# Strassen's scheme for the first expert product of an attention + mixture-of-experts kernel

## The chip, the cores and the metric

One core of a Trainium2 chip. The metric is the device time of one execution in microseconds: median 1120.63 of three runs (1118.05 to 1121.13) for the kernel before. Engines are named as in the profile: PE (matmul) with its weight loads PEld, DVE (vector), ACT (scalar), POOL (GpSimd, which also issues the indirect transfers) and SP (which issues the plain ones).

## What is computed

Attention (8 batches, 8 heads, 576 positions, 64 wide; four heads with a window of 32, four with a dilated one) gives x, 4608 tokens of 512. A gate with noise picks the best two of eight experts for each token, and the experts' outputs are added with the two weights:

```python
for e in range(E):
    for k in range(2):
        mask = top2[:, k] == e
        if not mask.any():
            continue
        h = np.maximum(x[mask] @ w1[e], 0.0)
        out[mask] += top2_w[mask, k, None] * (h @ w2[e])
```

w1[e] is 512 x 1024, w2[e] is 1024 x 512, all float32. "First product" below is x @ w1, "second product" is h @ w2.

## The kernel before, in words

**Stages.** The attention, the gate and the lists of tokens take the first 235 us or so and are not touched, but for the place where the first expert's weights are prepared. Then come the experts one after the other, the fullest first, with fixed capacities of 1216 (three experts), 1184 (two) and 1152 rows (three): nine tiles of 128 rows, and 64, 32 or no rows more. A loop at the end, which runs only if an expert overflows its capacity, is not entered here.

**Precision.** Each float32 operand is split into a high part that the fast float32 matmul reads (fp32r) and a low part, the difference. ACT makes the high part by a cast, DVE the low part by a subtraction. A product is three matmuls: high x high, high x low, low x high.

**First product** (`up`, L814). An expert's rows stand in three blocks of 384, 512 and the remaining 256 to 320 rows. For each block and each of eight groups of 128 hidden columns, twelve matmuls (4 slices of the inner dimension x 3) go into one bank of PSUM, tile `up`, of which there are three. Then ACT rectifies it into `hh` (L818) and DVE makes `hl` (L820; L823 for a last partial tile).

**Second product** (`down_tile`, L856). For each tile of 128 rows, 24 matmuls of 512 columns (8 x 3) into tile `dn`; DVE scales it by the token's weight into `y` (L865), POOL adds it to the output rows by an indirect transfer (L833).

**The rows of x.** POOL gathers them tile by tile (L758 for expert 0, L766 for the others, four gathers a tile); PE (`xrp`, L780, expert 0) or DVE (`xr`, L783) transposes; ACT casts (L785), DVE subtracts (L786). **Weights** come over SP into two staging buffers `ws` (L686 W1, L700 W2, 512 KB a transfer), ACT casts (L694, L707), DVE subtracts (L696, L709).

**What sets the order.** Each engine runs its instructions in the order in which the program wrote them. The program keeps a clock of its own, `now`, which `tick` moves on by the columns of the matmuls just written; `plan(t, f)` writes a piece of side work when the clock has passed t. So gathers, casts and loads stand between the matmuls' follow-up work at places worked out from this clock. The order of blocks is by hand: first products of one expert and second products of the one before alternate. Slots of expert 0 are dealt out in three parts, SPLITS = (0, 384, 896): the first 384 slots are filled from the first half of the tokens, the next up to 896 after the third quarter, and the rest at the end, so that expert 0 can begin early.

Of the kernel before, what the change touches and what calls it, by code (L numbers as in the profile page):

```python
# [35 lines left out]
NWARM = 24  # L36
SL_W1 = 5
# [9 lines left out]
def attention_moe_kernel(ctx, tc, qt, kp, kd, vpl, vdl, w_gate, w_noise, noise, w1, w2, out, CAPS=(1216, 1216, 1216, 1184, 1184, 1152, 1152, 1152), SPLITS=(0, 384, 896)):  # L47
# [13 lines left out]
    NBL = [max(bl[i][3] for bl in BLS) for i in range(3)]  # L61
# [11 lines left out]
    gp_ = ctx.enter_context(tc.tile_pool(name="gp", bufs=4))  # L73
# [180 lines left out]
    def setup_c():  # L254
# [3 lines left out]
        free = [late["stage"].tile([128, FF], I32, name="free", tag="ws") for _ in range(2)]  # L258
# [421 lines left out]
    ST = {}  # L680
    W1, W2 = {}, {}

    def stage_w1(e, kc):

        s = late["stage"].tile([128, FF], F32, name="ws", tag="ws")
        sync.dma_start(s, w1[0][128 * kc:128 * kc + 128] if type(e) is int else  # L686
                       row(w1, e).rearrange("(q c d) f -> c q d f", q=4, c=4)[kc])
        ST[1, kc] = s

    def split_w1(kc):  # L690
        s = ST.pop((1, kc))
        a = late["wp1"].tile([128, FF], F32R, name=f"w1h{kc}", tag=f"w1h{kc}")
        b = late["wp1"].tile([128, FF], F32R, name=f"w1l{kc}", tag=f"w1l{kc}")
        scalar.copy(a, s)  # L694
        W1[kc] = (a, b)
        return lambda: vector.tensor_tensor(b, s, a.bitcast(F32), op=OP.subtract)  # L696

    def stage_w2(e, fc):
        s = late["stage"].tile([128, 2, DM], F32, name="ws2", tag="ws")
        sync.dma_start(s, row(w2, e)[256 * fc:256 * fc + 256].rearrange("(c p) d -> p c d", p=128))  # L700
        ST[2, fc] = s

    def split_w2(fc):
        s = ST.pop((2, fc))
        a = late["wp2"].tile([128, 2, DM], F32R, name=f"w2h{fc}")
        b = late["wp2"].tile([128, 2, DM], F32R, name=f"w2l{fc}")
        scalar.copy(a, s)  # L707
        W2[fc] = (a, b)
        return lambda: vector.tensor_tensor(b, s, a.bitcast(F32), op=OP.subtract)  # L709
# [3 lines left out]
    def new_idx(e):  # L713
        if e == 0:
            ti = ixp.tile([128, nt, TC], I32, name="ixf", bufs=1)
            IX[0] = (ti, None, ti[:, :, 2:4])
            return
        t0 = ixp.tile([32, 4 * nt, 2], I32, name="ixt", bufs=2)
# [32 lines left out]
    def gather(e, t):  # L751
# [11 lines left out]
        if e != "o":  # L763
            pace()
# [6 lines left out]
    def xsplit(e, bi, t):  # L771
        r0, rn = TLS[e][t] if e != "o" else (0, 128)
        o = r0 - (BLS[e][bi][2] if e != "o" else 0)
        g = GT.pop((e, t))
        n = rn // 32
        xh, xl = X[e, bi]
        if e == 0:
            xr = gps.tile([128, 4, 128], F32, name="xrp", tag="tin")
            for c in range(4):
                tensor.transpose(xr[:, c, 0:rn], g[0:rn, c], ident[0:rn, 0:rn])  # L780
        else:
            xr = gp_.tile([128, 4, 128], F32, name="xr", tag="xr", bufs=2)
            vector.transpose(xr[:, :, 0:rn].rearrange("p c (g t) -> p g c t", t=32),  # L783
                             g[:, 0:n].rearrange("p g (c d) -> p g c d", d=32))
        scalar.copy(xh[:, :, o:o + rn], xr[:, :, 0:rn])  # L785
        return lambda: vector.tensor_tensor(xl[:, :, o:o + rn], xr[:, :, 0:rn], xh[:, :, o:o + rn].bitcast(F32),  # L786
                                            op=OP.subtract)

    def new_x(e, bi):
        pool = late["xp0" if bi == 0 else "xp"]  # L790
        t = pool.tile([128, 2, 4, NBL[bi]], F32R, name="x", tag="raw" if bi == 0 else f"x{bi}")
        X[e, bi] = (t[:, 0], t[:, 1])

    def plan_x(e, bi, t, step, lag):
        plan(t, lambda: new_x(e, bi))
        for i, ti in enumerate(range(BLS[e][bi][0], BLS[e][bi][1])):
            plan(t + step * i, lambda ti=ti: gather(e, ti))
            plan(t + step * i + lag, lambda ti=ti: xsplit(e, bi, ti), 1.2)

    HT = {}  # L800

    def up(key, X_, n, stacked):

        hh = late["hp"].tile([128, 8, 512], F32R, name="hh")
        hl = late["hp"].tile([128, 8, 512], F32R, name="hl")
        xh, xl = X_
        m = n - stacked
        for f in range(8):
            p = late["mps"].tile([128, 512], F32, name="up", tag="up", bufs=3)
            i = 0  # L810
            for kc in range(4):
                wh, wl = W1[kc]
                for a, b in ((wh, xh), (wh, xl), (wl, xh)):
                    tensor.matmul(p[:, 0:n], lhsT=a[:, 128 * f:128 * f + 128], rhs=b[:, kc, 0:n],  # L814
                                  start=(i == 0), stop=(i == 11))
                    i += 1
            tick(12 * n)
            scalar.activation(hh[:, f, 0:n], p[:, 0:n], AF.Relu)  # L818
            late["x"] = hh.bitcast(F32)[0:1, f, 0:1]
            vector.scalar_tensor_tensor(hl[:, f, 0:m], p[:, 0:m], 0.0, hh[:, f, 0:m].bitcast(F32),  # L820
                                        op0=OP.max, op1=OP.subtract)
            if stacked:
                vector.scalar_tensor_tensor(hh[:, f, n:n + stacked], p[:, m:n], 0.0, hh[:, f, m:n].bitcast(F32),  # L823
                                            op0=OP.max, op1=OP.subtract)
        HT[key] = (hh, hl)
# [15 lines left out]
    def down_tile(e, key, o, rn, t, sc, stacked):  # L841
        hh, hl = HT[key]
        p = late["mps"].tile([128, DM], F32, name="dn", tag="dn", bufs=2)
        y = late["yp"].tile([128, DM], F32, name="y")
        wsc = sc.bitcast(F32)[0:rn, t, 0:1]
        i = 0
        for f in range(8):
            wh, wl = W2[f // 2]
            if stacked:
                tensor.matmul(p[0:2 * rn], lhsT=hh[:, f, o:o + 2 * rn], rhs=wh[:, f % 2], start=(f == 0), stop=False,  # L850
                              skip_group_check=True)
                tensor.matmul(p[0:rn], lhsT=hh[:, f, o:o + rn], rhs=wl[:, f % 2], start=False, stop=(f == 7),
                              skip_group_check=True)
            else:
                for a, b in ((hh, wh), (hh, wl), (hl, wh)):
                    tensor.matmul(p[0:rn], lhsT=a[:, f, o:o + rn], rhs=b[:, f % 2], start=(i == 0), stop=(i == 23))  # L856
                    i += 1
            if f % 2 and f < 7:
                tick((2048, 3072)[not stacked])
# [4 lines left out]
        else:  # L864
            vector.tensor_scalar(y[0:rn], p[0:rn], wsc, None, op0=OP.mult)  # L865
        pend.append(scatter(e, y, rn, sc, t))

    def down(e, bi, a=0, b=9):

        t0, t1, s0, n = BLS[e][bi]  # L870
        sc = IX[e][2]
        for t in range(t0 + a, min(t0 + b, t1)):
# [349 lines left out]
```

## Time and profile before

| | |
|---|---|
| median of three runs | 1120.63 us |
| span of the profiled execution | 1109.4 us |
| PE busy, DVE, ACT, POOL | 1015.0, 463.9, 319.8, 527.7 us |
| first matmul of the first product | 235.7 us |
| first matmul of the second expert | 365.25 us |
| last matmul begins | 1099.36 us |

The profiled execution's time is known by its span, from its first to its last instruction, 1109.4 us; what lies around that is 11.2 us if it ran as long as the median. In the rows of a timeline stand the start, the length, the engine, the line, the operation, the tile written <- the tiles read, the shape and, in brackets, the idle time before it and what ended that. In the windows view each engine has its busy time with the number of instructions, and at the end of the row stand PE's granted clock, the share of the transfer engines and GB/s.

### The profile page before, as it was taken

The numbers are of one execution on the slowest core, as the hardware profiler recorded it, in microseconds if no ns is written. First come the engines' busy times: TensorE is split into PE (matmuls) and PEld (weight loads), VectorE is DVE, ScalarE is ACT, GpSimd is POOL, SyncE is SP. The second block draws the span as 40 slices with busy tenths as digits, with TensorE's granted clock in tenths as the row PEclk, the third lists the DMA queues.
The fourth block names the chain that finished last, engine by engine and source line by source line (L and its number), as shares of the span: only waits on it lengthen the run. The fifth ranks groups of instructions, "written<-read, shape, count | busy, mean of one in ns | idle before, by whom it ended". The sixth has DMA issues, their size and how long they took to land. (4 is left out here: it accounts for less than half of the span.)

```text
span 1109.4 us, 18401 instructions
## 1 busy us (share of the span) xinstructions
PE 1015.0 (91%) x7278; PEld 853.6 (77%) x7279; DVE 463.9 (42%) x1060; ACT 319.8 (29%) x612; POOL 527.7 (48%) x723
## 2 busy tenths in 40 slices
PE   5896776686999899999999999999999999999996
PEld 3774655465779789878988898788978898888885
DVE  6773535644224444334433433434343344333221
ACT  6673433531113232222222222212231213222110
POOL 6004243356866545664635564455456455553112
PEclk9998887887999999999999999999999999999999
DMA  7798687465243432633353334333433443353123
GB/s 275 254 345 292 193 270 251 122 205 161 44 90 76 102 101 48 139 60 103 65 117 68 97 72 101 82 79 85 97 83 81 104 68 102 62 129 58 32 30 46
DMA packets 77530, 132.91 MB, mean 120 GB/s; under 512 B 29968, under 2 KB 39616, under 8 KB 76160
## 3 DMA queue, kind: packets, MB, share of 16 engines
q1 hardware_dynamic: 55088, 92.55, 26.3%
q0 software_dynamic: 22352, 39.15, 19.6%
q8 instruction: 58, 0.95, 0.4%
q14 instruction: 32, 0.26, 0.1%
HBM read 92.11 MB, written 39.54 MB: 119 GB/s over the span
## 5 line engine op out<-in xcount | busy, mean ns | idle before, releaser
L814 PE MATMUL up<-x,w1h 128*128 128x512 f32 (+4 forms) x1536 | 397.5, 345 | 8.8 <-DVE hl L820 5.8
L766 POOL DMA_INDIRECT g<-xs,ixi x258 | 264.5, 1025 | 84.5 <-issue 79.1
L814 PEld LDWEIGHTS up<-x,w1h 128*128 128x128 f32 x1536 | 272.7, 189 | 36.4 <-DVE hl L820 7.6
L814 PE MATMUL up<-x,w1l 128*128 128x384 f32 (+4 forms) x768 | 264.1, 344 | 1.8 <-DVE w1l L696 1.1
L856 PE MATMUL dn<-w2h,hh 128*128 128x512 f32 x576 | 226.7, 394 | 2.0 <-DVE y L865 1.3
L856 PE MATMUL dn<-w2h,hl 128*128 128x512 f32 x576 | 225.3, 391 | 1.1 <-issue 1.1
L856 PE MATMUL dn<-w2l,hh 128*128 128x512 f32 x576 | 225.5, 391 | 0.6 <-issue 0.6
L820 DVE SCALAR_TENSOR_TENSOR hl<-up,hh 128x384 fp32r<-128x384 f32 (+2 forms) x192 | 106.1, 556 | 228.0 <-ACT hh L818 177.1
L833 POOL DMA_INDIRECT out_rows<-y,ixs x67 | 107.8, 1609 | 189.3 <-DVE y L865 158.3
L818 ACT ACTIVATE hh<-up 128x384 fp32r<-128x384 f32 (+4 forms) x192 | 94.2, 498 | 274.7 <-PE up L814 193.9
L814 PEld LDWEIGHTS up<-x,w1l 128*128 128x128 f32 x768 | 145.7, 190 | 14.7 <-DVE w1l L696 1.8
L856 PEld LDWEIGHTS dn<-w2h,hh 128*128 128x128 f32 x576 | 109.0, 189 | 25.6 <-DVE y L865 2.4
L856 PEld LDWEIGHTS dn<-w2h,hl 128*128 128x128 f32 x576 | 108.8, 189 | 24.0 <-issue 1.1
L856 PEld LDWEIGHTS dn<-w2l,hh 128*128 128x128 f32 x576 | 109.0, 189 | 22.6 <-issue 0.8
L865 DVE TENSOR_SCALAR y<-dn,ixs 128x512 f32<-128x512 f32 x63 | 46.9, 748 | 143.4 <-PE dn L856 114.9
L785 ACT CAST x<-xr 128x512 fp32r<-128x512 f32 x67 | 40.5, 605 | 189.9 <-DVE xr L783 158.5
L619 POOL DMA_INDIRECT tab<-en,si x72 | 72.2, 1002 | 30.7 <-issue 16.4
L696 DVE TENSOR_TENSOR w1l<-ws,w1h 128x1024 fp32r<-128x1024 f32 x32 | 38.8, 1217 | 94.8 <-ACT w1h L694 61.6
L297 POOL COPY spacer<-hh 1x1 f32<-1x1 f32 x72 | 24.2, 336 | 102.0 <-ACT hh L818 101.7
L694 ACT CAST w1h<-ws 128x1024 fp32r<-128x1024 f32 x32 | 33.0, 1048 | 115.9 <-DMA ws<-in_moe_w 115.8
L786 DVE TENSOR_TENSOR x<-xr,x 128x512 fp32r<-128x512 f32 x67 | 44.7, 666 | 18.0 <-ACT x L785 15.9
L783 DVE STREAM_TRANSPOSE xr<-g 128x512 f32<-128x512 f32 x67 | 45.7, 682 | 0.0
(184 smaller groups left out, 856.0 us busy)
## 6 DMA issues: line engine op xcount, KB each, us to landing
ws<-in_moe_w SPq DMA_DIRECT2D x64, 512.0 KB
out_rows<-zero SPq DMA_DIRECT2D x38, 256.0 KB
vd<-in_vdl SPq DMA_DIRECT2D x24, 390.0 KB
vp<-in_vpl SPq DMA_DIRECT2D x16, 585.0 KB
qt<-in_qt SPq DMA_DIRECT2D x14, 576.0 KB
xs<-x SPq DMA_DIRECT2D x24, 256.0 KB
kt<-in_kd SPq DMA_DIRECT2D x16, 320.0 KB
g<-xs,ixi POOLq DMA_INDIRECT x258
```

Of the source, the lines that this page charges most:

```text
L619: ins = gpsimd.indirect_dma_start(out=tab, out_offset=bass.IndirectOffsetOnAxis(ap=si[:, kq, t:t + 1], axis=0), in_=en[:, kq, t], in_offse ...
L696: return lambda: vector.tensor_tensor(b, s, a.bitcast(F32), op=OP.subtract)
L766: gpsimd.indirect_dma_start(out=g[:, j], out_offset=None, in_=xq, in_offset=bass.IndirectOffsetOnAxis(ap=IX[e][1][:, r0 // 32 + j:r0 // 32 ...
L783: vector.transpose(xr[:, :, 0:rn].rearrange("p c (g t) -> p g c t", t=32), g[:, 0:n].rearrange("p g (c d) -> p g c d", d=32))
L785: scalar.copy(xh[:, :, o:o + rn], xr[:, :, 0:rn])
L786: return lambda: vector.tensor_tensor(xl[:, :, o:o + rn], xr[:, :, 0:rn], xh[:, :, o:o + rn].bitcast(F32), op=OP.subtract)
L814: tensor.matmul(p[:, 0:n], lhsT=a[:, 128 * f:128 * f + 128], rhs=b[:, kc, 0:n], start=(i == 0), stop=(i == 11))
L818: scalar.activation(hh[:, f, 0:n], p[:, 0:n], AF.Relu)
L820: vector.scalar_tensor_tensor(hl[:, f, 0:m], p[:, 0:m], 0.0, hh[:, f, 0:m].bitcast(F32), op0=OP.max, op1=OP.subtract)
L833: ins = gpsimd.indirect_dma_start(out=out, out_offset=bass.IndirectOffsetOnAxis(ap=sc[0:rn, t, 1:2], axis=0), in_=y[0:rn], in_offset=None, ...
L856: tensor.matmul(p[0:rn], lhsT=a[:, f, o:o + rn], rhs=b[:, f % 2], start=(i == 0), stop=(i == 23))
L865: vector.tensor_scalar(y[0:rn], p[0:rn], wsc, None, op0=OP.mult)
```

## The change

An expert's rows now stand in two blocks: 640 rows (five tiles, NA = 5) and the rest (576, 544 or 512). For each block the first product is made by a form of Strassen's scheme: x is cut in two by rows within each tile (64 and 64) and in two along the inner dimension, w1 in two along the inner dimension and in two along the hidden one. Seven products of the halves stand in place of eight. Each product has two inner slices of 128 and the three precision terms: a group of six matmuls over half of the block's rows (320, 288, 272 or 256 columns). The hidden dimension is done in four steps j, each of which makes two groups of 128 hidden columns, f = j and j + 4.

**Sums of operands.** `sums_w1` makes the sums of a W1 quarter slice in place on DVE, four instructions of 128 columns, ahead of cast and subtraction, which are now over 896 columns (7 x 128) instead of 1024; a transfer is 256 KB. The host lays w1 out in these pieces. `xprep` does the same for a tile of x: four instructions of 2 x 64 columns on DVE; cast and subtraction are over 14 x 64 columns instead of 4 x 128. For expert 0 ACT copies the transposed tile to SBUF first.

```diff
+    def sums_w1(w, j, kk, eng):
+        s = ST[w, j, kk]
+        a = s[:, 0:512].rearrange("p (i h f) -> p i h f", i=2, h=2)
+        b = s[:, 512:896].rearrange("p (o f) -> p o f", o=3)
+        eng.tensor_tensor(b[:, 0], a[:, 1, 0], a[:, 1, 1], op=OP.add)
+        eng.tensor_tensor(b[:, 1], b[:, 0], a[:, 0, 0], op=OP.subtract)
+        eng.tensor_tensor(b[:, 2], a[:, 0, 1], b[:, 1], op=OP.subtract)
+        eng.tensor_tensor(a[:, 1, 0], a[:, 0, 0], a[:, 1, 0], op=OP.subtract)
...
+        vector.tensor_tensor(b[:, 0], q[:, 0, :, 1], q[:, 0, :, 0], op=OP.subtract)
+        vector.tensor_tensor(b[:, 1], q[:, 1, :, 1], b[:, 0], op=OP.subtract)
+        vector.tensor_tensor(b4, q[:, 1, :, 0], b[:, 1], op=OP.subtract)
+        vector.tensor_tensor(q[:, 0, :, 1], q[:, 1, :, 1], q[:, 0, :, 1], op=OP.subtract)
```

**Results.** A step uses a PSUM accumulator P (tile `up`, or `upg` from another pool in every second step of experts 1 to 7) and two more banks, `u0` and `u1`, each a tile of its own. P is read after its first group, after the sixth product's group and once more after each later group; ACT copies these into `su` and `m5`, DVE adds the other banks. ACT rectifies, DVE subtracts, as before. A step's last two groups are written among the next step's, and in each step the sixth product (P, slots 5) stands ahead of the fourth (P of the step before, slots 3 and 6):

```diff
+        for j in range(5):
+            i = j - 1
+            if i >= 0:
+                vector.tensor_tensor(SU[i][:, 1], SU[i][:, 1], RQ.pop((i, 1)), op=OP.add)
+                high(i, None, SU[i])
...
+                mm(P[j], j, 0, 0, True)
+            if i >= 0:
+                low(i, None, SU.pop(i))
+            if j < 4:
+                scalar.copy(SU[j][:, 0], P[j])
+            if i >= 0:
+                mm(P[i], i, 2, 2, False)
+                vector.tensor_tensor(M5[i], M5[i], P[i], op=OP.add)
+                high(i + 4, 1, M5[i])
+            if j < 4:
+                mm(RQ[j, 1], j, 4, 4, True)
+            else:
+                part()
+            if i >= 0:
+                low(i + 4, 1, M5.pop(i))
+            if j < 4:
+                scalar.copy(M5[j], RQ[j, 1])
+                mm(RQ[j, 0], j, 1, 1, True)
+                vector.tensor_tensor(SU[j][:, 0], SU[j][:, 0], RQ.pop((j, 0)), op=OP.add)
+                mm(P[j], j, 5, 5, False)
...
+                scalar.copy(SU[j][:, 1], P[j])
+            else:
+                part()
+            if i >= 0:
+                mm(P[i], i, 3, 6, False)
...
+                high(i + 4, 0, P[i])
+            if j < 4:
+                mm(RQ[j, 1], j, 6, 3, False)
+            else:
+                part()
+            if i >= 0:
+                low(i + 4, 0, P.pop(i))
```

`part` writes a quarter of the block's first down tile. After `up` the rest of the block's second product follows directly, so first and second products of the same block now alternate. There is one buffer for x and one for h; a block's x is cast when the first product before it is through. The scaling of y moves from DVE to ACT.

**Side work** runs in lanes, generators that wait for conditions of the program's clock: two for the weights (each loads 256 KB, writes the sums 5 us later, waits until the quarter's last matmul has been written, casts, subtracts), one each for gathers, x sums, x casts and index lists. The clock moves on after three matmuls, half a product's group. SPLITS is (0, 384, 640):

```diff
-            if bi == 0:
-                later(max(L0 + SL_W1 + 4 - slot[0], 3), lambda t=t: split_first(0, t))
+            if t < NA:
+                later(max(L0 + SL_W1 + 4 - slot[0], 3), lambda t=t: first_split(t))
...
+                stage_w1(EID[e], e, j, kk)
+                yield now[0] + US_LOAD
+                sums_w1(e, j, kk, vector)
+                yield now[0] + 1.5
+                if e:
+                    yield lambda e=e, j=j: free1.get(j, -1) >= e - 1
+                low = split_w1(e, j, kk)
+                yield now[0] + 1.2
+                low()
```

How the instructions stand, at three places. On PE, at the beginning of the first expert: `gt` belongs to the last gate, `xrp` are transposes of x, `up` is the first product. Before:

```order
L462 MATMUL pp_173<-xt,wg 32x64 x4
L500 MATMUL gt<-ident,gs 128x128 x3
L814 MATMUL up<-x,w1h_2863 128x384 x2
L814 MATMUL up<-x,w1l_2864 128x384
L814 MATMUL up<-x,w1h_2930 128x384 x2
```

and after:

```order
L500 MATMUL gt<-ident,gs 128x128 x3
L806 MATMUL xrp<-ident,g 128x128 x8
L573 LDWEIGHTS tri
L573 MATMUL posp<-ob,tri 128x48
...
L576 MATMUL posp<-ob,ones 128x8
L854 MATMUL up<-x,w_0_2867 128x320 x6
L854 MATMUL u_3480<-x,w_0_2867 128x320 x6
```

The transposes of tiles 3 and 4, and a part of the gate, now stand ahead of the first product.

On PE, a step in the second block of the fourth expert (272 columns); before, its third block (288 columns) is a run of groups of three, each twelve to a bank, as in the fence above. After:

```order
L854 MATMUL up<-x,w_2_6747 128x272 x6
L854 MATMUL upg<-x,w_1_6648 128x272 x6
L854 MATMUL u_7582<-x,w_2_6747 128x272 x6
L854 MATMUL u_7581<-x,w_2_6747 128x272 x6
L854 MATMUL up<-x,w_2_6747 128x272 x6
L854 MATMUL upg<-x,w_1_6648 128x272 x6
L854 MATMUL u_7582<-x,w_2_6747 128x272 x6
```

Seven groups make a step; `up` with w_2 is this step's accumulator, `upg` with w_1 that of the step before, `u_7582` and `u_7581` are the banks u1 and u0.

On DVE, at the same place: `hl`, `hh` and `h` are the hidden rows, `su` and `m` the sums, `w_0` the next expert's W1. Before:

```order
L820 SCALAR_TENSOR_TENSOR hl<-up,hh 128x256
L823 SCALAR_TENSOR_TENSOR hh<-up,hh 128x32
L820 SCALAR_TENSOR_TENSOR hl<-up,hh 128x256
L823 SCALAR_TENSOR_TENSOR hh<-up,hh 128x32
L783 STREAM_TRANSPOSE xr<-g 128x4x4x32
```

and after:

```order
L889 TENSOR_TENSOR su<-su,u_7499 128x272
L876 SCALAR_TENSOR_TENSOR h<-su,h 128x4x64 x2
L879 SCALAR_TENSOR_TENSOR h<-su,h 128x32
L712 TENSOR_TENSOR w_0_7569<-ws,w_0_7569 128x7x128 x2
L907 TENSOR_TENSOR m_7501<-m_7501,upg 128x272
L876 SCALAR_TENSOR_TENSOR h<-m_7501,h 128x4x64
L879 SCALAR_TENSOR_TENSOR h<-m_7501,h 128x16
```

Two instructions for a group of hidden columns have become a chain of adds and subtractions, and the low parts of the next W1 stand within it, ahead of the add to `m`.

More of the change, by code (lines that the diff above doesn't have):

```diff
@@ L678, in row @@
         return w[e] if isinstance(e, int) else w[bass.ds(e, 1)].rearrange("o a b -> (o a) b")
[L680 to L709, printed above, removed]
+    def stage():
+        return late["stage"].tile([128, 896], F32, name="ws", tag="ws")
@@ new lines, in split_w1, with low @@
+    def split_w1(w, j, kk):
+        s = ST.pop((w, j, kk)).rearrange("p (o f) -> p o f", o=7)
+        if (w, j) not in W1:
+            W1[w, j] = late["wp1" if j < 2 else "wp1b"].tile([128, 2, 7, 2, 128], F32R, name=f"w1_{j}", tag=f"w1_{j}")
+            ready1[w, j] = 0
+        t = W1[w, j]
+        scalar.copy(t[:, 0, :, kk], s)
+        def low():
+            vector.tensor_tensor(t[:, 1, :, kk], s, t[:, 0, :, kk].bitcast(F32), op=OP.subtract)
+            ready1[w, j] += 1
+        return low
@@ new lines, in attention_moe_kernel, with stage_w2, split_w2, low @@
+    ready1, ready2 = {}, {}
+    def stage_w2(e, w, f, where=None):
+        s = ST[w, f] = (where or stage)()[:, 0:512]
+        sync.dma_start(s, row(w2, e)[128 * f:128 * f + 128])
+    def split_w2(w, f):
+        s = ST.pop((w, f))
+        a = late["wp2"].tile([128, DM], F32R, name=f"w2h{f}")
+        b = late["wp2"].tile([128, DM], F32R, name=f"w2l{f}")
+        scalar.copy(a, s)
+        def low():
+            vector.tensor_tensor(b, s, a.bitcast(F32), op=OP.subtract)
+            W2[w, f] = (a, b)
+        return low
@@ new lines, in first_w2, with gathers @@
+    def first_w2(fs):
+        held_g[0] += 1
+        for f in fs:
+            stage_w2(0, 0, f, lambda: gp_.tile([128, 4, 128], F32, name="g").rearrange("p a b -> p (a b)"))
+            yield now[0] + US_LOAD
+            low = split_w2(0, f)
+            yield now[0] + 0.9
+            low()
+            yield now[0] + 0.3
+        held_g[0] -= 1
+    def gathers():
+        for e in range(1, E):
+            yield lambda e=e: e in index
+            for t in range(len(TLS[e])):
+                yield lambda: held_g[0] < 3
+                gather(e, t)
+                got[e, t] = now[0]
+                held_g[0] += 1
+                yield now[0] + US_GATHER
@@ new lines, in indices, with rest_of_slots @@
+    def indices():
+        for e in range(1, E):
+            yield lambda e=e: (e - 1, 0) in begun
+            yield now[0] + (42 if e == 1 else 24)
+            new_idx(e)
+            idx_dma(e, 0, CAPS[e])
+            yield now[0] + (12 if e == 1 else 9)
+            idx_copy(e, 0, CAPS[e])
+            index.add(e)
+            yield now[0] + 0.5
+    def rest_of_slots():
+        n = 0
+        while backlog:
+            pace(n % 4 == 0)
+            backlog.pop(0)()
+            n += 1
+            yield 1
@@ new lines, in attention_moe_kernel @@
+    plan(36, drain)
+    plan(36.1, numbers)
+    while done.get((0, 0), 0) < NA:
+        some()
+        tick(1200)
+    for fs in ((0, 1), (4, 5), (2, 6)):
+        go(first_w2(fs))
+    for g in (gathers(), preps(), splits(), indices()):
+        go(g)
+    for e in range(E):
+        for bi in range(2):
+            t0, t1, _, n = BLS[e][bi]
+            while done.get((e, bi), 0) < t1 - t0:
+                tick(600)
+            begun.add((e, bi))
+            first = down_gen(e, bi, t0)
+            up(e, bi, n, first)
+            down(e, bi, first)
```

424 lines of the change are left out of this document (243 added, 181 removed).

## The prediction

> **What bounds the kernel now.** I read the page's first part, then the stretches of the expert part (the windows view), then PE's timeline.
>
> ```profile
> span 1109.4 us, 18401 instructions
> PE 1015.0 (91%) x7278; PEld 853.6 (77%) x7279; DVE 463.9 (42%) x1060; ACT 319.8 (29%) x612; POOL 527.7 (48%) x723
> 235.70:260.20 24.50, 19.57 (x110) 19.09 (x109) 13.53 (x77) 5.94 (x13) 18.09 (x28) 0.86 0.84 271
> 260.20:286.10 25.90, 21.63 (x91) 16.94 (x90) 11.59 (x40) 4.54 (x8) 14.44 (x24) 0.87 0.40 103
> 367.00:1100.00 733.00, 722.29 (x3583) 622.05 (x3583) 284.55 (x453) 171.72 (x289) 364.41 (x453) 1.00 0.38 82
> ```
>
> From 367 to 1100 us PE is busy for 722 of 733 us at full clock (the 1.00), DVE for 285 and ACT for 172. So experts 1 to 7 last as long as PE needs for its matmuls, and a matmul fewer shortens the end as long as nobody makes PE wait. The first expert, from 235.7 us, is different: 0.86 of the clock, and gaps.
>
> ```profile
> 387.05 0.63 PE L814 MATMUL up<-x,w1h 128*128 128x512 f32 x2
> ...
> 387.75 0.63 PE L814 MATMUL up<-x,w1h 128*128 128x512 f32 x2
> 383.23 0.51 PE L814 MATMUL up<-x,w1h 128*128 128x384 f32 x2
> ...
> 383.75 0.51 PE L814 MATMUL up<-x,w1h 128*128 128x384 f32 x2
> 332.00 0.46 PE L814 MATMUL up<-x,w1h 128*128 128x320 f32 x2
> ...
> 332.44 0.45 PE L814 MATMUL up<-x,w1h 128*128 128x320 f32 x2
> 903.19 0.39 PE L856 MATMUL dn<-w2l,hh 128*128 128x512 f32 x1
> ...
> 903.87 0.39 PE L856 MATMUL dn<-w2l,hh 128*128 128x512 f32 x1
> ```
>
> A matmul's own duration overlaps the next, so its price is the distance of starts. Three matmuls lie between the rows of each pair: 0.70 us at 512 columns, 0.52 at 384, 0.44 at 320, so 233, 173.3 and 146.7 ns each; 226.7 in the second product. From 320 to 384 a column costs 0.416 ns, and 13.3 ns are left over per matmul. That gives, as estimates, 133.3, 126.7 and 120.0 ns at 288, 272 and 256 columns.
>
> **The matmuls that go.**
>
> ```profile
> L814 PE MATMUL up<-x,w1h 128*128 128x512 f32 (+4 forms) x1536 | 397.5, 345 | 8.8 <-DVE hl L820 5.8
> L814 PE MATMUL up<-x,w1l 128*128 128x384 f32 (+4 forms) x768 | 264.1, 344 | 1.8 <-DVE w1l L696 1.1
> ```
>
> Before: 2304 matmuls, 96 for each of 24 blocks. Eight blocks of 512 and eight of 384 columns take 8 x 96 x (0.2333 + 0.1733) = 312.3 us; the third blocks (three of 320, two of 288, three of 256) take 96 x 1.067 = 102.4 us: 414.7 us. After: 16 blocks of 4 steps x 7 products x 6 matmuls = 168, over half the columns. First blocks: 8 x 168 x 0.1467 = 197.2 us; second blocks (288 three times, 272 twice, 256 three times): 168 x 1.013 = 170.2 us; 367.4 us. PE's issue falls by **47.3 us**, 6.1 of it in the first expert. (Columns alone would give an eighth of 379 us, 47.4 us; 384 more matmuls cost 5.1 us, and the dearer 512-wide pitch goes.) The second product keeps its count.
>
> Those 13.3 ns per matmul come from the rows. The Trainium skill ("TensorE: Matmul & The Clock Gate", Back-to-back issue gap) gives a warm gap of N/2.4 + 2.5 ns for a single matmul; by it the 384 additional ones would cost 1 us, not 5. The trace's larger floor decides.
>
> **What DVE and ACT get in exchange.** Durations from the groups kept apart by shape:
>
> ```profile
> L820 DVE SCALAR_TENSOR_TENSOR hl<-up,hh 128x256 fp32r<-128x256 f32 x64 | 27.0, 423 | 63.6 <-ACT hh L818 51.1 <-issue 12.2
> L823 DVE SCALAR_TENSOR_TENSOR hh<-up,hh 128x32 fp32r<-128x32 f32 x16 | 2.9, 179 | 0.0
> L786 DVE TENSOR_TENSOR x<-xr,x 128x512 fp32r<-128x512 f32 x63 | 43.3, 687 | 18.0 <-ACT x L785 15.9 <-issue 2.1
> L696 DVE TENSOR_TENSOR w1l<-ws,w1h 128x1024 fp32r<-128x1024 f32 x32 | 38.8, 1217 | 94.8 <-ACT w1h L694 61.6 <-issue 33.1
> L818 ACT ACTIVATE hh<-up 128x512 fp32r<-128x512 f32 x64 | 37.8, 595 | 73.6 <-PE up L814 60.5 <-issue 8.7 <-remote 4.4
> L818 ACT ACTIVATE hh<-up 128x256 fp32r<-128x256 f32 x24 | 9.0, 383 | 43.1 <-PE up L814 40.1 <-issue 2.0 <-remote 1.1
> L694 ACT CAST w1h<-ws 128x1024 fp32r<-128x1024 f32 x32 | 33.0, 1048 | 115.9 <-DMA ws<-in_moe_w 115.8
> 919.65 0.60 ACT L818 ACTIVATE hh<-up 128x512 fp32r<-128x512 f32 x1 [1.20 <-PE up L814]
> 920.28 0.69 DVE L820 SCALAR_TENSOR_TENSOR hl<-up,hh 128x512 fp32r<-128x512 f32 x1 [0.30 <-ACT hh L818]
> 605.03 0.69 DVE L820 SCALAR_TENSOR_TENSOR hl<-up,hh 128x512 fp32r<-128x512 f32 x1 [1.68 <-ACT hh L818]
> 605.64 1.22 DVE L709 TENSOR_TENSOR w2l<-ws,w2h 128x1024 fp32r<-128x1024 f32 x1
> ```
>
> DVE costs about 0.14 us + 1.07 ns a column, ACT about 0.17 us + 0.83 ns; ACT hands to DVE in 0.03 us (920.25 to 920.28), and two DVE instructions in a row overlap by 0.08 us (0.61 between starts of one that lasts 0.69).
>
> One step at 272 columns is a ring of hand-overs: DVE adds the u1 bank (0.43), ACT rectifies 544 columns (0.8 with the remainder), DVE subtracts (0.8), DVE adds the second product's sum to m5 (0.43), ACT rectifies, copies twice and rectifies again (1.6), DVE subtracts (0.45) and is back at the add: about 4.6 us with the hand-overs, against 7 x 6 x 0.1267 = 5.3 us of PE. So the step fits with 0.7 us to spare; at 320 columns it has 1.6 us. PE's cover is thin but there, and each bank is rewritten three products after it was filled (about 2.3 us).
>
> The rest lands in second blocks, where the next expert's W1 is prepared. Counting the order with these prices less the overlap: DVE has 11 us of step work there and about 8.8 more (24 sums of 128 columns at 0.2, or 16 and one tile of X, and four subtractions of 896 at 1.02). From the first add to the last subtraction PE has 25 products of 0.76 and two quarters of a down tile (6 x 0.2267 each), 21.7 us: DVE is 91% full. First blocks: 11.3 + 3.6 in 24.7 us. Two places stand in PE's way. In one step both low parts of W1's first quarter (2 x 1.02 us) stand on DVE between the subtractions and the m5 add, and the group that next writes that accumulator waits for the add: 2.0 - 0.7 = 1.3 us; two casts of W1 on ACT (0.93 each) ahead of the same step's rectification push the add by another 0.4 or so. In the last step two casts (1.86 us) stand on ACT ahead of the copy that lets PE go on in its accumulator: 1.86 - 0.7, about 1.2 us. Together **3 us for each of seven second blocks, +21** (at least 1 us each if casts hide; 8.8 if nothing hides), and 0.5 us for each first block, **+4** (0 to 8). The sums of X, its casts and the scaling of y that moves to ACT stand beside the second product, which needs neither; the next X has 18 to 23 us there for about 16 us of DVE.
>
> What goes: PE's waits for the three `up` buffers.
>
> ```profile
>   DVE hl L820: 13.4, 10
> ```
>
> Of these 13.4 us (PE and weight loads, ten waits), I take **-8**; 0 to -13.
>
> **The start.** The first block is now 640 rows, so PE also needs tiles 3 and 4.
>
> ```profile
> 235.70 0.60 PE L814 MATMUL up<-x,w1h 128*128 128x384 f32 x2
> 238.32 1.00 POOL L758 DMA_INDIRECT g<-xs,ixf  x1 [6.96 <-DMA ws<-in_moe_w]
> 242.16 0.96 POOL L758 DMA_INDIRECT g<-xs,ixf  x1 [0.30 <-issue]
> 253.70 0.20 PE L573 MATMUL posp<-ob,tri 128*128 128x24 bf16 x1 [4.93 <-DVE ob L558]
> 365.25 0.51 PE L814 MATMUL up<-x,w1h 128*128 128x384 f32 x2
> ```
>
> Their four gathers run from 238.3 to 243.1; copy, four sums, cast and subtraction take 0.6 + 4 x 0.28 + 0.9 + 1.1 = 3.7 us by the prices above, and for landing and transposing, which no row prices here, I take 2 (0 to 6): the first matmul comes at about 249 instead of 235.7, 13 us later, on the path. Against it: from 235.7 to 286.1 PE has 96 x 0.1733 + 72 x 0.2267 = 33 us of matmuls in 50.4 us, so 17 us are waits (4.93 for the gate at 253.7) and half clock after them, and a later start meets fewer. I let 5 come back: **+8** (0 to +20; a gain only if more than the 13 us came back).
>
> **Sum.** -47.3 + 21 + 4 - 8 + 8 = -22.3 us. The tail behind the last matmul stays. The span is 1109.4 us, 11.2 under the median of 1120.63, and I keep that distance: **1098 us**.
>
> **Rivals.** *The queues hide it all*: ring and slack hold, the casts fall into ACT's idle time, the start costs little: -47.3 + 7 + 0 - 8 + 4 = -44, 1076 us. For it: DVE is only 42% busy. *DVE bounds second blocks*: sums, low parts and casts are covered only by the first 2 to 3 us, so 6 us per block: 21 becomes 42, 1119 us. For it: 91% full in order, so a late operand is not made up. *Slower: the W1 loads land late.*
>
> ```profile
> 549.94 2.30 SPq L686 DMA_DIRECT2D ws<-in_moe_w  x2
> 561.47 1.05 ACT L694 CAST w1h<-ws 128x1024 fp32r<-128x1024 f32 x1 [11.05 <-DMA ws<-in_moe_w]
> 499.82 3.42 SPq L700 DMA_DIRECT2D ws<-in_moe_w  x2
> 503.63 1.05 ACT L707 CAST w2h<-ws 128x1024 fp32r<-128x1024 f32 x1 [1.55 <-DMA ws<-in_moe_w]
> ```
>
> The new sums sit on DVE, planned 5 us behind their load, and everything PE waits for is queued behind them. W1 pairs took 11 us to land, W2 pairs 4. If the halved pairs still took 11, DVE would stand 6 us in each second block and 3 in the X behind it: 7 x 9 = 63, 1161 us; the sign turns at 3.7 us per expert (26 of gain and bound, over seven), a landing at about 8 us. Against it: half the bytes, and the index loads no longer follow directly. *POOL falls behind.*
>
> ```profile
> 550.46 1.22 DVE L696 TENSOR_TENSOR w1l<-ws,w1h 128x1024 fp32r<-128x1024 f32 x1
> 550.54 2.02 POOL L766 DMA_INDIRECT g<-xs,ixi  x1 [0.26 <-issue]
> L766 POOL DMA_INDIRECT g<-xs,ixi x258: 940/955/2016, 314.9 to 1005.1; - x129
> ```
>
> A gather beside a DVE instruction with two SBUF inputs took 2.02 us instead of 0.955, and the change triples such DVE time. An expert has 37 gathers; with gaps of 0.3 us and its scatters POOL needs some 66 us, and 105 if all were held so, over the 97 us that PE then needs: 7 x 8 = 56, 1154 us. It decides from 0.84 us more per gather in the mean. The Trainium skill ("SBUF — State Buffer", Who interferes with whom) says that such a DVE instruction shares a read port with GpSimd instructions that read SBUF, exclusively; this pair of rows agrees. A change that does not do what it says can be ruled out: the order has 28 groups of six matmuls per block.
>
> **Chances.** Forecast 0.53, all hidden 0.20, DVE bounds 0.13 (1119 lies on the edge: half of it faster, half same), late loads 0.09, POOL 0.05. 0.3% is about what a measurement here tells from no change: 3.4 us. Faster 0.53 + 0.20 + 0.06 = 0.79, same 0.06, slower 0.15 (the last two and 0.01 of DVE's). Range: 1070 (six below "all hidden", as the 13 us waits and 7 us have ends) to 1122 (past "DVE bounds"); it leaves out the two slow cases and 0.03 below.
>
> **What would show it.** Right: 2688 `up` and `u` matmuls with 880 ns per group of six at 320 columns; PE waits for ACT and DVE of 2 to 4 us in each second block, at the m5 add and the copy behind the casts, nearly none in first blocks; first expert matmul at 247 to 251; DVE at 60 to 70% of the span. Wrong: gaps before first blocks of an expert (X late), POOL busy without gaps, DVE idle on `ws`, or pitches above 146.7 ns.

## The result, and the profile after

The changed kernel takes 1255.25 us (median of four runs, 1253.69 to 1260.36) against 1120.88 for the kernel before beside it (four runs): a ratio of 1.122, interval 1.117 to 1.127. It is 134 us slower, where 22 us less were forecast. The profiled executions differ by 1252.5 - 1109.4 = 143.1 us; a run of the changed kernel takes 1.8 us beyond its span (1254.3 and 1252.5), so the profiled execution of before was a quicker one than its median, and its distance of 11.2 us from the median wasn't time around the span.

The page's first lines and the clock's row, after:

```profile
span 1252.5 us, 20794 instructions
PE 1026.3 (82%) x7662; PEld 879.5 (70%) x7663; DVE 702.9 (56%) x1892; ACT 501.9 (40%) x1010; POOL 528.0 (42%) x723
PEclk9997986777989897989799979998999799979998
```

No engine is near its limit. DVE has 239 us more, but stands at 56%; PE has fallen from 91% to 82%, and the clock, which stood at full speed in experts 1 to 7, now dips again and again. Cut at the first matmul of the first product and at the second expert's first one (L854), the two executions stand so:

| us | before | after | difference |
|---|---|---|---|
| start to first matmul of first product | 235.70 | 256.28 | +20.6 |
| first expert | 129.55 | 148.03 | +18.5 |
| experts 1 to 7 and the tail | 744.15 | 848.19 | +104.0 |

The windows view of experts 1 to 7 (last columns: granted clock, share of the transfer engines, GB/s), and PE's groups for the first product:

```profile
406.00:1242.00 836.00, 725.98 (x3919) 640.25 (x3918) 470.66 (x1116) 316.95 (x614) 364.53 (x453) 0.93 0.35 72
```
```profile
L854 PE MATMUL u<-x,w 128*128 128x320 f32 (+3 forms) x1152 | 199.1, 322 | 48.6 <-issue 22.9 <-DVE su L889 20.4 <-ACT m L916 4.0
L854 PE MATMUL up<-x,w 128*128 128x320 f32 (+3 forms) x864 | 159.6, 327 | 60.7 <-issue 21.8 <-ACT su L922 12.7 <-DVE m L907 7.7
L854 PE MATMUL upg<-x,w 128*128 128x320 f32 (+3 forms) x672 | 117.4, 313 | 33.6 <-DVE m L907 9.9 <-issue 9.2 <-ACT su L922 8.2
```

PE stands idle for 110 of these 836 us, and in all 142.9 us before matmuls of the first product (10.6 before). Part of it is put down to DVE and ACT, part to nothing that the profile shows ("issue"). But DVE and ACT were not late with work of their own. The waits view gives what they waited for (us in total, times, longest):

```profile
ACT su L922 <- remote: 50.0, 9, 6.7
DVE su L889 <- remote: 39.5, 6, 8.7
DVE m L907 <- remote: 20.9, 5, 6.5
ACT su L904 <- remote: 14.3, 3, 5.8
```

"remote" is a signal for which the view finds no instruction that ended when it came. These four lines read PSUM tiles that only PE writes; their other operands come from DVE and ACT themselves, whose instructions the view would name. So the signal is PE's, and the two engines together waited 124.7 us for it.

**One place.** The second block of expert 4, windows view and the timelines of PE, ACT, DVE and POOL:

```profile
695.30:720.00 24.70, 24.70 (x112) 20.46 (x111) 11.48 (x26) 6.90 (x10) 14.01 (x20) 1.00 0.32 51
720.00:731.00 11.00, 5.38 (x38) 4.72 (x37) 2.14 (x6) 1.84 (x4) 8.56 (x11) 0.96 0.35 67
731.00:742.00 11.00, 5.82 (x23) 5.18 (x24) 2.16 (x7) 1.55 (x5) 6.74 (x9) 0.50 0.32 60
742.00:752.00 10.00, 8.80 (x61) 8.32 (x60) 7.81 (x25) 5.45 (x16) 0.00 (x0) 0.91 0.19 49
...
1201.00:1223.50 22.50, 22.50 (x180) 21.98 (x179) 10.16 (x27) 9.86 (x24) 1.61 (x2) 1.00 0.10 13
```
```profile
722.92 1.02 PE L854 MATMUL up<-x,w 128*128 128x272 f32 x6 [0.54 <-ACT su L904]
724.37 1.01 PE L854 MATMUL u<-x,w 128*128 128x272 f32 x6 [0.43 <-ACT m L916]
725.22 0.91 PE L854 MATMUL upg<-x,w 128*128 128x272 f32 x6
730.79 1.73 PE L854 MATMUL up<-x,w 128*128 128x272 f32 x6 [4.66 <-issue]
735.92 3.09 PE L854 MATMUL u<-x,w 128*128 128x272 f32 x12 [3.41 <-DVE su L889]
```
```profile
730.35 0.39 ACT L922 COPY su<-up 128x272 f32<-128x272 f32 x1 [6.03 <-remote]
740.35 0.39 ACT L904 COPY su<-upg 128x272 f32<-128x272 f32 x1 [3.69 <-PE u L854]
```
```profile
735.43 0.44 DVE L889 TENSOR_TENSOR su<-su,u 128x272 f32<-128x272 f32 x1 [6.36 <-remote]
```
```profile
728.32 1.03 POOL L788 DMA_INDIRECT g<-xs,ixi  x1 [0.30 <-issue]
729.66 0.94 POOL L788 DMA_INDIRECT g<-xs,ixi  x1 [0.30 <-issue]
...
738.12 0.94 POOL L788 DMA_INDIRECT g<-xs,ixi  x1 [0.31 <-issue]
```

The group at 722.92 has its last matmul five pitches of 0.147 us later, at about 723.65; the copy that reads it starts at 730.35, 6.7 us later, on an ACT that was idle. The group at 724.37 is read by DVE at 735.43, 10.3 us after its last start, and the one at 725.22 at 740.35, 14.5 us after. The readers aren't the late ones: in the trace's record of semaphore updates, on which the views rest, the semaphore that PE's matmuls raise goes up for these three groups at 730.33, 735.34 and 740.32, and the readers start within 0.1 us of it. Meanwhile PE has nothing that it may write, and in the next stretch its clock is 0.50. POOL issues look-ups of rows (indirect gathers) with 0.3 us between them, but for a scatter at 732, until 739.06; from 742 on all engines run as if nothing had been. The last row of the windows is the last expert's second block, where POOL has next to nothing to do: PE is busy for all of its 22.5 us. The same step there (PE, then ACT):

```profile
1200.99 0.87 PE L854 MATMUL up<-x,w 128*128 128x256 f32 x6
```
```profile
1201.90 0.37 ACT L904 COPY su<-up 128x256 f32<-128x256 f32 x1
```

Last start at 1201.58, read at 1201.90: 0.32 us. So in this place PE's word that a product is ready came late where POOL's look-ups stand close together. In the kernel before POOL read an element of the newest hidden rows ahead of each tile's gathers (`pace()`), and most tiles were planned 9 us apart; the diff takes the reading away and plans them 4.8 us apart. Neither was costed in the prediction:

```diff
         if e != "o":
-            pace()
+            gpsimd.memset(spacer, 0.0)
...
-            plan_x(e, 2, start + 2, 9, LAG)
...
+                yield now[0] + US_GATHER
```

On POOL's timeline of before, three tiles in a row begin their gathers at 601.99, 613.04 and 622.59; after, at 722.03, 727.08 and 734.08.

### The profile page after: what moved, and what is told of

It reads as the page before. It is cut to its first block, busy times and chain, and to the rows that moved or that the text cites. A ratio compares the mean times of both kernels' runs of the same rounds, so it can differ in the third digit from the quotient of the medians.

```text
span 1252.5 us, 20794 instructions
## 1 busy us (share of the span) xinstructions
PE 1026.3 (82%) x7662; PEld 879.5 (70%) x7663; DVE 702.9 (56%) x1892; ACT 501.9 (40%) x1010; POOL 528.0 (42%) x723
## 3 DMA queue, kind: packets, MB, share of 16 engines
q0 software_dynamic: 22352, 39.15, 18.0%
## 5 line engine op out<-in xcount | busy, mean ns | idle before, releaser
L969 PE MATMUL dn<-w2h,h 128*128 128x512 f32 x1152 | 365.4, 394 | 2.8 <-DVE h L876 2.8
L788 POOL DMA_INDIRECT g<-xs,ixi x258 | 266.1, 1031 | 85.4 <-issue 70.1
L969 PEld LDWEIGHTS dn<-w2h,h 128*128 128x128 f32 x1152 | 218.2, 190 | 48.9 <-DVE h L876 4.3
L854 PE MATMUL u<-x,w 128*128 128x320 f32 (+3 forms) x1152 | 199.1, 322 | 48.6 <-issue 22.9
L969 PE MATMUL dn<-w2l,h 128*128 128x512 f32 x576 | 226.3, 393 | 0.0
L854 PEld LDWEIGHTS u<-x,w 128*128 128x128 f32 x1152 | 180.3, 208 | 55.5 <-issue 26.2
L854 PE MATMUL up<-x,w 128*128 128x320 f32 (+3 forms) x864 | 159.6, 327 | 60.7 <-issue 21.8
L854 PEld LDWEIGHTS up<-x,w 128*128 128x128 f32 x864 | 139.3, 210 | 71.3 <-issue 24.5
L854 PE MATMUL upg<-x,w 128*128 128x320 f32 (+3 forms) x672 | 117.4, 313 | 33.6 <-DVE m L907 9.9
L854 PEld LDWEIGHTS upg<-x,w 128*128 128x128 f32 x672 | 101.2, 197 | 42.7 <-DVE m L907 13.7
L969 PEld LDWEIGHTS dn<-w2l,h 128*128 128x128 f32 x576 | 109.2, 190 | 21.5
L619 POOL DMA_INDIRECT tab<-en,si x72 | 71.8, 997 | 38.7 <-issue 16.3
L709 ACT CAST w<-ws 128x896 fp32r<-128x896 f32 x64 | 58.2, 941 | 17.6 <-DVE ws L701 13.1
```

What stands on the lines that cost most here:

```text
L619: ins = gpsimd.indirect_dma_start(out=tab, out_offset=bass.IndirectOffsetOnAxis(ap=si[:, kq, t:t + 1], axis=0), in_=en[:, kq, t], in_offse ...
L709: scalar.copy(t[:, 0, :, kk], s)
L788: gpsimd.indirect_dma_start(out=g[:, j], out_offset=None, in_=xq, in_offset=bass.IndirectOffsetOnAxis(ap=IX[e][1][:, r0 // 32 + j:r0 // 32 ...
L854: tensor.matmul(p, lhsT=w[:, y, a, kk], rhs=x[:, z, SLOTS[b][kk], 0:N], start=start and kk == 0 and i == 0, stop=kk == 1 and i == 2, skip_ ...
L969: tensor.matmul(p[0:rn], lhsT=h[:, a, f, r0:r0 + rn], rhs=b, start=(i == 0), stop=(i == 23), skip_group_check=True)
```

## The experiments

e1 to e4, e6 and e11 are one run each. e1 and e6 leave out the choice of rows, e2 and e11 the sums of W1 for experts 1 to 7.

**The theory (A):** look-ups that POOL issues back to back hold back PE's signals; Strassen's ring of hand-overs needs one for every product, so it stands still. **Rivals:** DVE's sums hold the ring (B); the bytes of the gathers, or loads, are in the way (C).

**e1: rows in order, as plain transfers on SP.**

```diff
-            gpsimd.memset(spacer, 0.0)
+            for j in range(rn // 32):
+                sync.dma_start(g[:, j], xq[128 * j:128 * j + 128])
+            GT[e, t] = g
+            return
```

> Leaves out the choice of rows: for experts 1 to 7 the four gathers of a tile on POOL become four plain transfers of the same size on SP, of rows in order (the wrong ones); everything else stays. Theory A (PE's completion signals come late while POOL issues gathers back to back; in the changed kernel a copy on ACT read a finished group 6 to 15 us after its last matmul began, 0.3 us in the last block, where POOL is idle): the signals come 0.3 us after, second blocks of experts 1 to 6 fall from 43 to 23 to 27 us, first blocks from 30 to 41 to 29 to 31, so 1255 - 6 x 17 - 25 = 1128 us (1105 to 1145). Theory B (DVE bounds the second blocks, by the sums and low parts of W1): POOL has no part in it, 1240 to 1260. Theory C (the bytes of the gathers hold PE up, whoever issues them): same bytes, 1240 to 1260.

Measured: 1125.98 us (before beside it 1125.97, also one run). The stalls are gone with the look-ups, though the bytes are the same; C falls.

**e2: W1's sums left out for experts 1 to 7.**

```diff
-                sums_w1(e, j, kk, vector)
+                if e == 0:
+                    sums_w1(e, j, kk, vector)
```

> Leaves out the sums of W1 for experts 1 to 7 (three of the seven slices are copies of others): DVE loses 32 sums of 0.29 us per expert, 9.3 us, and gets 8 x 0.15 more for a subtraction in two parts; the gathers stay. Theory A (late completion signals beside gathers): the stalls stay, at most 10 us less, 1240 to 1258. Theory B (DVE bounds the second blocks): 7 x 8 = 56 us less, about 1200. Theory C (bytes of the gathers): as A.

Measured: 1233.93 us. DVE falls by 47 us (702.9 to 655.7), the time by 21; by ratios, 1.096 to the kernel before beside it against 1.122, by 29. That lies below what A expected (1240 to 1258) and far above what B did (about 1200): the sums explain a quarter of the loss at most.

**e3: the old pacing alone, restored.**

```diff
-            gpsimd.memset(spacer, 0.0)
+            pace()
...
+            o = 64 if m == 1 else 0
+            late["x"] = ht.bitcast(F32)[0:1, 0, f, o:o + 1]
```

> Undoes one part of the change: before a tile's four gathers POOL again reads one element of the hidden rows written last, where the change put a memset that waits for nothing. The four gathers of a tile still follow each other and the next tile is planned 4.8 us later, so POOL can still issue them nearly without gaps where buffers are free. Theory A: fewer in a run, some of the stall goes: 1170 to 1245. Theory B and C: 1250 to 1260.

Measured: 1211.57 us. By ratios (1.076 against 1.122) over a third of the loss comes back: first to last `up` of a second block takes 36 to 39 us instead of 42 to 44 (28 to 29 in e1). The four gathers of a tile still stand back to back, and the tiles are still planned 4.8 us apart. What that plan costs by itself was not run.

**e4: each gather on its own, paced, 2.0 us apart,** and the index lists loaded 18 us sooner.

```diff
-US_GATHER = 4.8
+US_GATHER = 2.0
...
+                for j in range(TLS[e][t][1] // 32):
+                    gather(e, t, j)
```

> The same gathers, one by one: each waits for the hidden rows or the y written last, planned 2.0 us apart on the program's clock, the index lists loaded 18 us earlier. Theory A, that a run of gathers without gaps is what delays the signals: lags under 3 us, second blocks 25 to 31 us, 1130 to 1175. If each gather delays the signals by a fixed amount wherever it stands: about as many stalls, 1220 to 1260. Theory B and C: 1245 to 1260.

Measured: 1142.61 us, with the same look-ups and bytes as the changed kernel. Second blocks take 28 to 30 us as in e1. Of what is left, the second expert's rows come late: 16 us of PE's time ahead of its first block.

**e5: the kernel before, with its pacing taken away.**

```diff
-            pace()
+            gpsimd.memset(spacer, 0.0)
```

> The one part alone, in the kernel before: POOL no longer reads an element of the hidden rows written last ahead of a tile's gathers, so that they run in a row as soon as buffers and index lists are there. Theory A (runs of gathers delay PE's completion signals): the signals come late here too, but three banks of twelve matmuls cover some 5 us of it; the worst runs show: 5 to 40 us slower, 1126 to 1160. If the pacing plays no part: no change, 1118 to 1126.

Measured: 1146.87 against 1111.84, a ratio of 1.033 (1.026 to 1.040). Groups of before without pacing:

```profile
L814 PE MATMUL up<-x,w1h 128*128 128x512 f32 (+4 forms) x1536 | 408.6, 352 | 32.9 <-DVE hh L823 13.7 <-DVE hl L820 12.2 <-issue 6.1
```

The idle time there was 8.8 us. So the same line costs 3.3% where PE has three banks of twelve matmuls to go on with; in the changed kernel it is worth 0.046 of the time of before (e3), on top of the closer plan. That the ring, in which each product waits for an earlier one's reader, makes lateness dearer is argued from this and not shown: in e5 readers wait 85.2 us for such signals, 61.8 more than before, and the time grows by 35; in the changed kernel they wait 124.7 us, and it grows by 134.

**e6: plain transfers again, but issued by POOL.**

```diff
-            gpsimd.memset(spacer, 0.0)
+            for j in range(rn // 32):
+                gpsimd.dma_start(out=g[:, j], in_=xq[128 * j:128 * j + 128])
+            GT[e, t] = g
+            return
```

> As the first experiment (rows in order, the wrong ones), but the plain transfers are issued by POOL in place of SP. If any transfer that POOL issues delays PE's signals: as the changed kernel, 1225 to 1265. If only the look-up of rows by an index list does: as with SP, 1110 to 1145.

Measured: 1119.09 us (before 1111.84). Its group, beside that of the changed kernel:

```profile
L787 POOL DMA_DIRECT2D g<-xs x258 | 169.0, 1049 | 17.4 <-DVE xr L812 14.1 <-DMA out_rows<-y,ixs 2.4 <-issue 0.8
```
```profile
L788 POOL DMA_INDIRECT g<-xs,ixi x258 | 266.1, 1031 | 85.4 <-issue 70.1
```

As many transfers from the same engine, as long each and closer together (258 x 1.049 = 271 us of them overlap into 169), through the same queue (q0, 22352 packets and 39.15 MB in both), and next to no lag: of the four waits of the result two are left, 4.8 us in all.

```profile
DVE m L910 <- remote: 2.9, 1, 2.9
DVE su L892 <- remote: 1.9, 1, 1.9
```

So it needs the look-up, not POOL's being busy. One thing isn't separated: e1 and e6 read rows that lie next to each other, the look-ups rows that lie scattered.

The attention part of e6 has both cases beside each other, since POOL writes the slots of tokens there by an index list (`tab`, L619; in the kernel before too). DVE's maximum reads what 48 matmuls of PE wrote, twice the same step:

```profile
115.58 1.52 PE L362 MATMUL s<-kt,qt 128*32 128x128 f32 x48
121.58 1.52 PE L362 MATMUL s<-kt,qt 128*32 128x128 f32 x48
```
```profile
117.16 0.96 DVE L367 TENSOR_REDUCE mx<-s 128x12 f32<-128x768 f32 x1 [1.03 <-PE s L362]
127.99 0.96 DVE L367 TENSOR_REDUCE mx<-s 128x12 f32<-128x768 f32 x1 [5.80 <-remote]
```
```profile
122.28 0.97 POOL L619 DMA_INDIRECT tab<-en,si  x1 [0.51 <-issue]
...
126.09 0.96 POOL L619 DMA_INDIRECT tab<-en,si  x1 [0.21 <-issue]
```

With POOL quiet (it issues nothing from 110.4 to 121.6) DVE starts 0.06 us after the matmuls' end at 117.10. Beside four indirect writes it starts 4.9 us after their end at 123.10, and 0.9 us after the last write's. So writes by an index list do it as well, and the kernel before has the same: 20.9 us for this line (`mx`) in its waits view.

**e7, e8: e4 with the second expert's rows sooner** (its gathers 1.1 us apart) and W1's second half later (2.6 us at each quarter); e8 also with the fourth product ahead of the sixth.

```diff
+                    yield now[0] + 2.6 * kk
...
-                    yield now[0] + US_GATHER
+                    yield now[0] + (1.1 if e == 1 and t < NA else US_GATHER)
```

> The fourth experiment (gathers one by one, paced) with two mends: the second expert's first five tiles are gathered 1.1 us apart instead of 2.0, as PE waited 16 us for them, and the two lanes that prepare W1 and W2 stand 2.6 us apart, so that a cast and a subtraction of one quarter, not of two, stand ahead of the sums that PE waits for. Theory A with the prediction's two places in the second blocks: 13 us back before the second expert, and about half of the 4 to 5 us in each of seven second blocks: 1142.6 - 13 - 14 = 1116 (1105 to 1130). If the rest of the second blocks is something else: 1128.

> The seventh experiment with one part of the change undone: the fourth product stands ahead of the sixth again. Between the group that the sum into m5 reads and the fourth product's group stand two groups instead of three, and the same between the sixth and the next group in its bank: 0.8 us less cover in each step, in second blocks mostly: 64 steps, half of them short by about 0.5: 10 to 25 us slower than the seventh. If the ring has slack everywhere: no change.

Measured: 1170.73 and 1162.09 (before 1111.84), ratios 1.055 (1.048 to 1.062) and 1.045 (1.040 to 1.051). Both miss: e7 is slower than expected, and e8 is faster than e7, not slower. The delay adds up quarter by quarter in a lane that W2 shares, so W2 comes late and PE waits for it in the second product, as e7's waits view says:

```profile
PE dn L974 <- DVE w2l L729: 21.9, 8, 4.7
PE dn L974 <- ACT w2h L726: 17.7, 8, 3.8
```

The order of the products can't be read from a pair that waits for its weights.

**e9: the delay once per expert, loads planned 4.4 us instead of 5.0.** e10: e9 with the fourth product ahead of the sixth. e11: e9 without W1's sums in experts 1 to 7.

```diff
-US_LOAD = 5.0
+US_LOAD = 4.4
...
                 yield lambda e=e: (e - 1, 1) in begun
+                yield now[0] + 2.6 * kk
...
-                    yield now[0] + 2.6 * kk
```

> The seventh experiment without what made it slow: there the second lane of weights was moved on by 2.6 us at each of four quarters, W2 came late, and PE waited 3 to 7 us in each first block's second product (and ran at half clock after it). Now the lane is moved once per expert, and the plan counts 4.4 us for a load instead of 5.0. Theory A with the two places of the prediction: those 9 us in each of seven experts go, second blocks stay at 26.7 to 28.3: 1171 - 61 = 1110 (1102 to 1120). If W2 is late for another reason: 1135 or more.

> The ninth experiment with the fourth product ahead of the sixth again. The eighth was 8.6 us faster than the seventh, but there W2 stood in the way, and the order moved where it did. If the order counts by the cover it gives: 5 to 20 us slower than the ninth. If the eighth's difference was the order's own: 5 to 9 us faster. If the ring has slack: the same.

> Leaves out the sums of W1 for experts 1 to 7, as the second experiment did, on top of the ninth. If DVE's queue holds what is left of the second blocks (4 us in each of seven over their matmuls): 10 to 20 us less than the ninth. If the low parts and casts alone do: 0 to 6 less.

Measured beside 1114.69: e9 1117.85, ratio 1.0039 (1.0011 to 1.0067); e10 1125.16, ratio 1.0105 (1.0068 to 1.0142); e11 1107.17 in one run. Each lies in a range that was expected. The sixth product ahead of the fourth is worth about 7 us (0.0066 of 1115); the sums cost about 10. Experts 1 to 7 and PE's groups in e9:

```profile
386.00:1104.00 718.00, 696.02 (x3926) 615.64 (x3927) 465.38 (x1114) 315.30 (x613) 439.09 (x633) 1.00 0.40 83
```
```profile
L857 PE MATMUL u<-x,w 128*128 128x320 f32 (+3 forms) x1152 | 182.4, 303 | 8.3 <-DVE su L894 7.1 <-ACT m L921 1.1
L857 PE MATMUL up<-x,w 128*128 128x320 f32 (+3 forms) x864 | 148.7, 310 | 26.9 <-ACT x L829 10.0 <-DVE m L912 5.3 <-DVE h L881 5.0
L857 PE MATMUL upg<-x,w 128*128 128x320 f32 (+3 forms) x672 | 112.8, 303 | 10.6 <-DVE m L912 6.4 <-ACT su L909 3.1
```

PE's idle time before the first product is 45.8 us instead of 142.9, and the clock is 1.00. By the cuts of the result's table e9 has 253.43, 131.36 and 729.01 us: experts 1 to 7 are 15 us shorter than before, and the later start takes that and 4 more.

**e12: the first expert in three blocks** (384, 256 and the rest), so that it can begin early again.

```diff
+N0 = 3
...
+        cuts = ([0] if BLS else [0, N0]) + [NA, len(tl_)]
```

> The ninth experiment, with the first expert's rows in three blocks (384, 256 and the rest) instead of 640 and the rest, so that its first product needs three tiles, as in the kernel before. Theory S (the five tiles of the first block set the start, and what is lost there does not come back): first matmul at 234 to 244 instead of 253, and the second expert, which began at 384.8 (365.3 in the kernel before), 8 to 16 us earlier, after a price of 168 more matmuls x 13.3 ns = 2 us: 1118 - 12 = 1106 (1097 to 1113). If the first expert is held by its weights, the gate's last part or the gathers for the second expert: the first matmul comes earlier, the second expert at 380 or later, 1114 to 1122.

Measured: 1083.46 us; before on that chip 1049.64, so no time, only the ratio, compares with the others: 1.031 (1.028 to 1.034). A miss. The first matmul comes at 198.56, but W1's second half isn't there:

```profile
201.97 1.50 PE L859 MATMUL up<-x,w 128*128 128x192 f32 x12
203.31 1.50 PE L859 MATMUL u<-x,w 128*128 128x192 f32 x12
...
212.92 0.74 PE L859 MATMUL up<-x,w 128*128 128x192 f32 x2 [4.86 <-ACT w L711]
...
269.71 1.50 PE L859 MATMUL up<-x,w 128*128 128x128 f32 x12
271.05 1.50 PE L859 MATMUL u<-x,w 128*128 128x128 f32 x12
```

The first expert takes 159 us instead of 131, and narrow blocks are dear: twelve matmuls take 1.34 us at 192 and at 128 columns alike, 111.7 ns each, where the line of the prediction (13.3 ns + 0.416 ns a column) gives 93 and 67. None of the versions beat the kernel before. e9 is the nearest; e11 is quicker but leaves work out.

## Why the prediction was wrong, step by step

**PE's issue, -47.3: right.** PE's timeline, after:

```profile
561.69 1.04 PE L854 MATMUL upg<-x,w 128*128 128x320 f32 x6
562.57 1.04 PE L854 MATMUL up<-x,w 128*128 128x320 f32 x6
563.45 1.78 PE L854 MATMUL u<-x,w 128*128 128x320 f32 x11
```

0.88 us per group of six, and 2688 matmuls (1152 + 864 + 672), as forecast.

**The step that failed: "So the step fits with 0.7 us to spare", and "each bank is rewritten three products after it was filled (about 2.3 us)".** The ring was summed from durations of DVE and ACT and from hand-overs of some 0.03 us; the hand-over from PE was taken to be of that kind always. It is 0.32 us where POOL is quiet, and up to 14.5 us where it isn't. A cover of 2.3 us can't take that up. The prediction had sign, place and price of every operation on DVE and ACT and put what the diff did to the gathers, the wait taken away and the closer plan, at nothing. With the look-ups replaced by plain transfers the ratio is 1.000 on SP (e1) and 1.007 on POOL (e6), in one run each. With them kept, from the changed kernel to e9, the ratio falls from 1.122 to 1.004: that is 0.118 of 1120 us, about 132 us, nearly all of what was lost. (e9 changes the planning of W1's loads too; e4, which spreads the gathers and fetches their index lists sooner, is at 1.015 in single runs.)

The stalls then cost more than themselves, since the clock falls behind them: 0.50 from 731 to 742 us. The Trainium skill ("TensorE: Matmul & The Clock Gate", HAM oscillation — how this bites in real kernels) says that gaps of PE above some 3.4 us bring half speed; the gaps of 4.66 and 3.41 us ahead of and in that stretch agree.

**The rivals.** "POOL falls behind" had the right engine and the wrong way: gathers did not get longer (1031 ns in the mean, 1025 in the same group of before), and POOL was not late; it was too early. "The W1 loads land late" and "DVE bounds second blocks" were not it: e1 has the same loads and the same sums as the changed kernel, and lost nothing.

**The two places in second blocks: right, somewhat too small.** In e4, where the lag is away, DVE and PE:

```profile
789.31 2.08 DVE L712 TENSOR_TENSOR w<-ws,w 128x896 fp32r<-128x896 f32 x2
791.31 0.43 DVE L912 TENSOR_TENSOR m<-m,upg 128x272 f32<-128x272 f32 x1
```
```profile
791.80 1.02 PE L857 MATMUL upg<-x,w 128*128 128x272 f32 x6 [0.87 <-DVE m L912]
...
800.99 1.02 PE L857 MATMUL upg<-x,w 128*128 128x272 f32 x6 [0.71 <-ACT su L927]
```

Both low parts stand ahead of the m5 add, and the copy is late at the end of the block, as written. With small waits between them a second block has some 5 us over its matmuls instead of 3: in e4 28 to 30 us from the first `up` matmul to the last, where PE needs 22.5 at 256 columns (the block of the last expert, above) and by the pitches 23.6 and 24.7 at 272 and 288; 3.5 to 5.6 us in e9. First blocks of experts 1 to 7 took 27.9 to 33.1 us in e9, where the pitches give 27.4 (168 of 146.7 ns and 12 of 226.7): 0.5 to 5.7 us instead of 0.5, the most in the second expert, which begins at half clock behind a wait of 3.66 us for x. The waits of before for its `up` buffers went.

**The start, +8: mis-sized, and not by the late signals.** The first matmul came at 256.28, not 249, and nothing came back: e9's first expert takes 131.4 us against 129.55, though PE's issue for it was to be 6.1 us less. Its second expert begins at 384.79, 19.5 us later than before. With the first expert's share of PE's issue the prediction had +8 - 6.1 = +1.9 for that; so 17.6 us are off there. The term itself comes to 19.5 + 6.1 = 25.6 us, above its own upper end of 20. For experts 1 to 7 it had -47.3 + 6.1 + 21 + 4 - 8 = -24.2; e9 has -15.1, 9.1 off. Together that is e9's span of 1113.8 in place of 1109.4 - 22.3. So without the lag most of the forecast gain would have been lost by the time the second expert begins.

**Still open.** Which part of the chip holds PE's signal while look-ups are issued is not settled. A matmul's record ends before its signal, and the semaphore's record shows only that the signal came late: the Trainium skill ("Perfetto Trace Analysis", Tensor Engine Instruction (MATMUL, LD_WEIGHTS)) says that a matmul's signal goes out when PSUM has acknowledged its writes, and that the profile's start is that of reading the data. So the rows can't tell a matmul that finished late from a signal that travelled late; the durations of about 1 us in the rows above show nothing of 14.5 us.

## What to carry to other kernels

A diff's removed waits have to be costed like its added work: ask of each what it kept apart. The time from a group's last matmul start to its first reader's start, taken beside and away from runs of look-ups, shows whether the hand-over from PE can be trusted; a scheme that needs it for every product wants the look-ups spread (here singly, 2 us apart and behind fresh results), or more banks between. And what a later start costs should be read as a date, the second expert's first matmul, not as a share that will come back.

## What the runs showed of the hardware

- PE's signals that a product is ready came up to 14.5 us after the product's last matmul had begun, beside indirect gathers that POOL issued 0.3 us apart; in the place shown three came one by one during the run, and the last four at 740.32 to 741.24, within 2.2 us of the last gather's end at 739.06. Indirect writes did it too: 4.9 us in the attention part of e6. Plain transfers issued by POOL as densely (e6) or by SP (e1) did not do it. The kernel before has the same in small: its waits view has

```profile
ACT hh L818 <- remote: 23.4, 6, 6.0
```

  with pacing, and without it, in e5,

```profile
ACT hh L818 <- remote: 85.2, 18, 9.2
```

  so 18 waits in place of 6. The Trainium skill ("SBUF — State Buffer", Who interferes with whom) says that DMA never contends with a compute engine. Where nothing waits that holds here too, since the pitch of the matmuls is the same (0.88 us for six at 320 columns); but the hand-over, which it doesn't speak of, is delayed.
- A matmul of these, with a weight load of its own, takes 111.7 ns at 192 and at 128 columns alike (e12, at full granted clock).
